# A new opening and a shifted order of reads for an attention block with a Fourier mixer on one core

## The chip, the core and the metric

The kernel runs on one core of a Trainium2 chip. A core has a matrix engine (TensorE, PE in the profile, with its weight loads as PEld), a vector engine (VectorE, DVE), an activation engine (ScalarE, ACT), GpSimd (POOL) and SyncE (SP), which here only issues DMAs. Each engine works through its own instructions in order and waits on semaphores for the others. The data lie in SBUF, matmul results in the eight banks of PSUM, inputs and output in HBM. The metric is the device time of one execution in microseconds (us); the time shown is the median of three runs.

## The reference

There are 8 batches, 8 heads, 512 tokens and 32 state rows of 64 features. Two cross attentions without projections come first: the tokens read the state, and the state reads the tokens. Their outputs, 544 rows per head, go through a real Fourier mix over rows and features, a layer norm without parameters, and a two-layer network with residual.

```python
scores = scale * x @ state.T;  a = softmax(scores);  xread = a @ state      # B, H, 512, D
scores2 = scale * state @ x.T; a2 = softmax(scores2); sread = a2 @ x         # B, H, 32, D
x = concat([xread, sread], axis=2) -> (B, 544, H*D = 512)
u = x + real(fft(fft(x, axis=1), axis=2))
un = (u - mean(u)) / sqrt(var(u) + 1e-6)
out = u + relu(un @ w_ch1) @ w_ch2            # w_ch1 512 x 2048, w_ch2 2048 x 512
```

Inputs and output are float32; the kernel computes its matmuls in bfloat16.

## The kernel before

**Stages of one batch.** `attend(b)` makes the two attentions in 13 steps: turn the state and x on PE (`turn_state`, `turn_x`), scores in both directions with an exponential on ACT (`scores_t`, `scores`), four `xread`s (one matmul pair, then a reciprocal and a multiply on DVE, line 304), `sread` (eight matmuls; a reciprocal; then eight 32-row multiplies that alternate between DVE, line 327, and ACT, line 329, all into the tile XR), `low` (the rows that are their own mirror or fall out of the symmetric blocks), and `fold` (sums and differences of a row and its mirror: Sm, XE, XO, XN). `transform(b)` makes the Fourier mix in 11 steps: four times `over_s` (matmuls with cosine and sine tables over the rows, line 378), two times `over_d` (matmuls with the table T2 over the features, line 391; DVE adds the residual into U), four times `centre` (statistics and subtraction on DVE, lines 233 and 402) and `turn_u` (transposes into unT, line 407). A block of 128 rows and its mirror are computed from the same matmuls; `r` is 0 for a block and 1 for its mirror. `layer1(b)` is 64 matmuls of 512 columns (line 482) with a Relu on ACT; `layer2(b)` is four tiles of 16 matmuls (line 500), each emptied by one DVE operation that scales by the row's standard deviation and adds the residual (`ot`, line 505) and then stored. A mirrored tile goes to a scratch tensor `r_dram` and from there, reversed, to the output (lines 512 and 513); the store waits for the scratch write. `low_rows` and the layers with the key `("L", g)` do the low rows of four batches at once.

**Order.** All five engines run in the order in which the Python code issues instructions. `weave` gives each stream of steps an interval of a stage, spreads the steps evenly over it and issues all by that position; where two are equal the earlier stream goes first. After an opening (tables, `attend(0)`, then `transform(0)` with `attend(1)`), stage `b` weaves `layer1(b)`, `layer2(b - 1)`, `transform(b + 1)` and all of `attend(b + 2)`. The casts of x to bfloat16 are on DVE for batch 0, ACT for batch 1 and POOL after that.

**Buffers.** PSUM has one buffer of two banks for the reads (`psX`, also for `sread`), three banks for all small matmuls (`psQ`), two for layer 1 (tag `ph`) and one for layer 2 (tag `po`); in the last stage every second tile of layer 2 takes a bank of `psQ`. x is loaded in float32 into two buffers `xs` by five DMAs on SyncE's queue; the bfloat16 copies `xin` have two buffers too. `ot` has three.

**Opening.** The tables are computed on DVE (`turn`: an angle reduced to one turn) and ACT (`Sin`), in tiles that share their space with hT. POOL copies the 32-row parts into CL and SL, sets constants in the tiles, and then issues the weight loads, which convert float32 to bfloat16, on a queue of its own (q0; SyncE's DMAs are q1):

```python
    nc.gpsimd.tensor_copy(gate, xs_of[0][:, :, 0])
    for q in range(4):
        nc.gpsimd.dma_start(out=w1[:, :, q * 512:(q + 1) * 512], in_=w1v[:, :, q * 512:(q + 1) * 512])
```

The copy into `gate` makes POOL, and so its loads, wait for x of batch 0.

## Time and profile before

| | |
|---|---|
| median of three runs | 403.11 us (402.58 to 403.5) |
| profiled execution | 403.93 us, of it the span of the trace 402.2 us |
| granted PE clock, mean | 0.939 |
| PE busy | 324.7 us (81%), 1971 matmuls |
| PE weight loads | 174.1 us (43%) |
| DVE busy | 186.7 us (46%) |
| ACT busy | 162.7 us (40%) |
| POOL busy | 60.8 us (15%) |
| HBM read, written | 21.51 MB, 13.11 MB |

Times within a trace count from the start of the span. The profile's page divides the span into 40 equal slices, so a slice is 10 us; a digit is the busy share in tenths. Matmuls are pipelined and their ends are modelled, so a busy PE need not be a PE at its peak. The granted clock (PEclk) is a mean over a window: 1.00 is 2.4 GHz, 0.50 is 1.2 GHz; before its first change it is written as 1.00. In a timeline or a group, `out<-in` names tiles; xin is x in bfloat16, xTp the transposed x in PSUM, xrp, xfp, xlp and srp the reads in PSUM, gp and yp the two transforms, ph and po the layers. A wait is put down to the instruction that released it.

### The profile page before, as it was taken

The numbers are of one execution on the slowest core, as the hardware profiler recorded it, in microseconds if no ns is written. First come the engines' busy times: TensorE is split into PE (matmuls) and PEld (weight loads), VectorE is DVE, ScalarE is ACT, GpSimd is POOL, SyncE is SP. The second block draws the span as 40 slices with busy tenths as digits, with TensorE's granted clock in tenths as the row PEclk, the third lists the DMA queues.
The fourth block names the chain that finished last, engine by engine and source line by source line (L and its number), as shares of the span: only waits on it lengthen the run. The fifth ranks groups of instructions, "written<-read, shape, count | busy, mean of one in ns | idle before, by whom it ended". The sixth has DMA issues, their size and how long they took to land.

```text
span 402.2 us, 5181 instructions
## 1 busy us (share of the span) xinstructions
PE 324.7 (81%) x1971; PEld 174.1 (43%) x2008; DVE 186.7 (46%) x426; ACT 162.7 (40%) x296; POOL 60.8 (15%) x134
## 2 busy tenths in 40 slices
PE   0245649769988998899899996999799999997900
PEld 0123425435544554455564553454445444553400
DVE  8936682683287138733773167415840722001110
ACT  2746326455544454445453523353444353430000
POOL 4680230130022002201220013001200200000000
PEclk9975758999999999999999999899999999999975
DMA  9489963000101610161015110101010111111121
GB/s 190 71 148 196 196 135 61 0 0 2 52 29 52 146 53 13 52 139 47 28 52 133 40 57 35 52 28 52 28 53 28 52 44 63 52 45 39 49 78 52
DMA packets 48744, 26.56 MB, mean 66 GB/s; under 512 B 36176, under 2 KB 44368, under 8 KB 48720
## 3 DMA queue, kind: packets, MB, share of 16 engines
...
q8 instruction: 15, 0.25, 0.3%
q14 instruction: 9, 0.07, 0.1%
HBM read 21.51 MB, written 13.11 MB: 86 GB/s over the span
## 4 chain that ended last, share of the span: by engine, by line
PE 55%; DVE 24%; POOL 4%; ACT 4%; issue 4%; DMA 3%; another core or an unknown queue 1%; SPq 1%; DVEq 0%; ACTq 0%; POOLq 0%
PE ph L482 22%; PE po L500 20%; DVE st L233 3%; PE gp L378 3%; DVE ub L402 3%; DMA out_dram<-ot 3%; DVE ot L505 2%; PE yp L391 2%; DVE XR L327 2%; ACT XR L329 2%; DVE XR L304 2%; PE eTp L276 2%; PE xTp L267 2%; DVE U L395 1%; DVE U L393 1%
## 5 line engine op out<-in xcount | busy, mean ns | idle before, releaser
L500 PE MATMUL po<-w,hT 128*128 128x512 bf16 x501 | 128.4, 381 | 6.2 <-DVE ot L505 5.5
L482 PE MATMUL ph<-unT,w 128*128 128x512 bf16 x491 | 131.0, 384 | 1.1 <-issue 0.2
L484 ACT ACTIVATE hT<-ph 128x512 bf16<-128x512 f32 x128 | 76.5, 597 | 98.0 <-PE ph L482 96.0
L500 PEld LDWEIGHTS <-hT 128*128 128x128 bf16 x512 | 50.2, 98 | 66.4 <-issue 9.1
L482 PEld LDWEIGHTS <-w 128*128 128x128 bf16 x640 | 56.2, 99 | 45.7 <-issue 2.2
L505 DVE SCALAR_TENSOR_TENSOR ot<-po,rstd,U 128x512 f32<-128x512 f32 x32 | 23.9, 750 | 75.1 <-PE po L500 68.0
L393 DVE TENSOR_TENSOR U<-yp,XR 128x511 f32<-128x511 f32 x16 | 10.9, 682 | 47.7 <-PE yp L391 47.7
L237 POOL TENSOR_TENSOR rstd<-mv,epst 128x1 f32<-128x1 f32 x34 | 7.1, 209 | 142.1 <-DVE mv L235 142.1
L409 ACT COPY unT<-tp 128x512 bf16<-128x512 bf16 x32 | 18.7, 584 | 22.1 <-PE tp L407 22.1
L300 PE MATMUL xfp<-stb,ET 128*128 128x260 bf16 x32 | 7.1, 307 | 20.6 <-ACT XR L329 14.2
L233 DVE BATCH_NORM_STATS2 st<-U 128x6 f32<-128x512 f32 x32 | 21.9, 686 | 0.2
L300 PEld LDWEIGHTS <-ET 128*128 128x128 bf16 x80 | 6.4, 100 | 35.7 <-issue 15.1
L385 POOL COPY GL<-G 128x128 bf16<-128x128 bf16 x8 | 2.4, 294 | 126.3 <-ACT G L383 126.3
L383 ACT CAST G<-gp 128x288 bf16<-128x288 f32 x32 | 12.8, 399 | 21.0 <-PE gp L378 15.3
L267 PE MATMUL xTp<-ident,xin 128*128 128x128 bf16 x128 | 11.7, 240 | 11.4 <-DVE xin L111 11.4
L238 POOL TENSOR_TENSOR rstd<-rstd,mhalf 128x1 f32<-128x1 f32 x34 | 20.4, 600 | 2.7
L329 ACT ACTIVATE XR<-srp,rcs 32x64 bf16<-32x64 f32 x32 | 9.9, 310 | 26.0 <-DVE XR L327 26.0
L402 DVE TENSOR_SCALAR ub<-U,mv 128x512 bf16<-128x512 f32 x32 | 16.4, 512 | 1.1
L391 PE MATMUL yp<-T,G 128*128 128x512 bf16 x61 | 16.3, 379 | 0.4 <-ACT E L292 0.2
L267 PEld LDWEIGHTS <-xin 128*128 128x128 bf16 x128 | 9.6, 108 | 14.7 <-DVE xin L111 12.5
L327 DVE TENSOR_SCALAR XR<-srp,rcs 32x64 bf16<-32x64 f32 x32 | 9.0, 281 | 9.9 <-ACT XR L329 9.6
L407 PE MATMUL tp<-ident,ub 128*128 128x128 bf16 x128 | 13.4, 231 | 0.0
...
## 6 DMA issues: line engine op xcount, KB each, us to landing
...
xs<-in_x_dram SPq DMA_DIRECT2D x8, 2.0 KB
```

Of the source, the lines that this page charges most:

```text
L233: nc.vector.bn_stats(st6, u)
L238: nc.gpsimd.tensor_tensor(rstd, rstd, mhalf, op=ALU.pow)
L267: nc.tensor.transpose(p[:, o:o + 128], xin[:, si, 1 + 128 * (2 * g + k):129 + 128 * (2 * g + k)], ident)
L327: nc.vector.tensor_scalar(o, in0=i, scalar1=rcs[ph, g:g + 1], scalar2=None, op0=ALU.mult)
L329: nc.scalar.activation(o, i, AF.Copy, scale=rcs[ph, g:g + 1])
L391: nc.tensor.matmul(yp, lhsT=G[:, c, 128 * k:128 * k + 128], rhs=T2[:, c, :], start=(c == 0), stop=(c == 3))
L402: nc.vector.tensor_scalar(t, in0=ud, scalar1=mv[:, 0:1], scalar2=None, op0=ALU.subtract)
L409: nc.scalar.copy(unT[:, :, col:col + 128], tp[:, 0:512].rearrange("p (a b) -> p a b", b=128))
L482: nc.tensor.matmul(ph[:, o:o + n], lhsT=w1[:, c, f * 128:(f + 1) * 128], rhs=un_of[key][:, c, :], start=(c == 0), stop=(c == DC - 1))
L484: nc.scalar.activation(hT[:, per * i:per * i + per, :].rearrange("p a b -> p (a b)"), ph, AF.Relu)
L500: nc.tensor.matmul(po, lhsT=h_of[key][:, f, i * 128:(i + 1) * 128], rhs=w2[:, f, :], start=(f == 0), stop=(f == FC - 1))
L505: nc.vector.scalar_tensor_tensor(ot, in0=po, scalar=rstd, in1=u, op0=ALU.mult, op1=ALU.add)
```

## The change

- **Weights and x.** POOL's work ahead of `gate` is other work: the table copies into CL and SL move to DVE, and the constants of the state tile move to POOL. x of batch 0 is cast on ACT, of every later batch on POOL. x of batch 2 is loaded after a small DVE copy that stands behind the reads of batch 0.
- **Tables.** The second table is computed for half of its columns only, in three parts that are woven into the opening (`second_turn` on DVE, `second_table` on ACT, `finish_tables` on DVE); the rest is copied with signs. A first `Sin` on a constant stands at the start.
- **Dummy matmuls.** `warm(n)` issues n matmuls of the identity with itself into a PSUM tile that nobody reads: 48 at the start, then 8, 4 or 2 after each step of batch 0's attention and transform.
- **Order.** `attend` returns its scores (seven steps) and its reads (six, with an empty step after `sread`) apart. Batch 1's scores are woven between batch 0's reads. In stage `b` the reads of batch `b + 2` take the first half and the scores of batch `b + 3` the second. Layer 2 is ahead of layer 1 at equal positions.
- **PSUM.** Layer 1, layer 2, the dummies and two of batch 0's reads share one tag `c` with three banks; `sread` uses two tiles of `psQ`, one for each half, with all of DVE's multiplies ahead of ACT's.
- **Layer 1 of batch 0** runs in two halves of 256 columns. Batches 0 and 1 are centred on ACT with the opposite sign, which the Relu's scale turns back.
- **The last batch** has its two mirrored tiles first in layer 2.

```diff
-    psF = ctx.enter_context(tc.tile_pool(name="psF", bufs=2, space=bass.MemoryType.PSUM))
+    psF = ctx.enter_context(tc.tile_pool(name="psF", bufs=3, space=bass.MemoryType.PSUM))
...
-    make_identity(nc, ident)
...
-    pi_ = singles.tile([128, 5], I32, name="pi_")
+    pi_ = singles.tile([128, 4], I32, name="pi_")
...
+    make_identity(nc, ident)
...
         xs, t = xs_of[b], xin_bufs[b % 2]
         if b == 0:
             for si in (0, 1, 3, 2):
-                nc.vector.tensor_copy(t[:, si, 1:513], xs[:, si, :])
-        elif b == 1:
-            for si in (0, 1, 3, 2):
                 nc.scalar.copy(t[:, si, 1:513], xs[:, si, :])
         else:
             nc.gpsimd.tensor_copy(t[:, :, 1:513], xs)
...
+    nc.gpsimd.memset(stb[:, 1:].rearrange("p b g c -> p (b g c)").bitcast(F32), 0.0)
...
-    def state_blocks(lo, hi):
+    def state_blocks(lo, hi, copy=nc.scalar.copy):
...
-            nc.scalar.copy(stb[pq, lo:hi, :, 4 + 64 * hh:68 + 64 * hh], stf[pq, lo:hi, :, :])
+            copy(stb[pq, lo:hi, :, 4 + 64 * hh:68 + 64 * hh], stf[pq, lo:hi, :, :])
...
+    gate = singles.tile([128, 4], F32, name="gate")
+    gate2 = singles.tile([128, 4], F32, name="gate2")
+    nc.vector.memset(gate2, 0.0)
+    nc.scalar.activation(gate2[:, 1:2], gate2[:, 0:1], AF.Sin)
     state_ones(0, 1)
     state_blocks(0, 1)
+    cast_x(0)
...
+    nc.vector.memset(CL.rearrange("p a b -> p (a b)"), 0.0)
+    nc.vector.memset(SL.rearrange("p a b -> p (a b)"), 0.0)
...
+        nc.vector.scalar_tensor_tensor(q, in0=f, scalar=-1.0, in1=f, op0=ALU.mult, op1=ALU.max)
...
+    turned = []
+    def second_turn():
+        nc.vector.tensor_copy(l2, li)
+        turned.extend(turn(dm, dm, l2, [3], gen2))
+    def second_table():
+        f2, q2_ = turned
+        w = 2.0 * PI / dm * shrink
+        nc.scalar.activation(T2[:, 0, :], q2_[:, 0, :], AF.Sin, bias=halfpi, scale=-w)
+        nc.scalar.activation(T2[:, 2, :], f2[:, 0, :], AF.Sin, bias=0.0, scale=-w)
+        nc.scalar.activation(gate2[:, 3:4], gate2[:, 0:1], AF.Exp)
+    def finish_tables():
+        c4 = [T2[:, i, :].rearrange("p (n r) -> p r n", r=4) for i in range(4)]
+        for o, classes in ((1, ((0, 1.0), (2, 1.0), (0, -1.0), (2, -1.0))), (3, ((2, 1.0), (0, -1.0), (2, -1.0), (0, 1.0)))):
+            for r, (i, sign) in enumerate(classes):
+                nc.vector.tensor_scalar(c4[o][:, r, :], in0=c4[i][:, r, :], scalar1=sign, scalar2=None, op0=ALU.mult)
+        alt = T2[0:1, 2, :].rearrange("p (n two) -> p two n", two=2)
+        nc.vector.memset(alt[:, 0, :], 1.0)
+        nc.vector.memset(alt[:, 1, :], -1.0)
+        for hh in range(4):
+            pq = slice(32 * hh, 32 * hh + 32)
+            nc.vector.tensor_copy(CL[pq, hh, :], cl1[pq])
+            nc.vector.tensor_copy(SL[pq, hh, :], sl1[pq])
...
-            (nc.vector.tensor_copy if g == 0 else nc.scalar.copy)(
+            (nc.vector.tensor_copy if g == 0 or b == 0 else nc.scalar.copy)(
...
-        def xread(c0, rev, name, o, ps=slice(0, 128)):
-            p = x2(name)
+        def xread(c0, rev, name, o, ps=slice(0, 128), apart=False):
+            n = ps.stop - ps.start
+            p = None if apart else x2(name)
+            rs = wk.tile([128, 2, 4], F32, name="rs", tag="rs", bufs=4)
+            ov = o.rearrange("p (g h d) -> p g h d", g=2, d=D)
             for half in range(2):
                 g = 1 - half if rev else half
                 rhs = sb[:, g, 259::-1] if rev else sb[:, g, 4:264]
-                nc.tensor.matmul(p[:, half, 0:260], lhsT=ET[:, g, c0:c0 + 128], rhs=rhs, start=True, stop=True)
-            n = ps.stop - ps.start
-            rs = wk.tile([128, 2, 4], F32, name="rs", tag="rs", bufs=4)
+                ph = psF.tile([128, 512], F32, name=name, tag="c") if apart else p[:, half]
+                nc.tensor.matmul(ph[:, 0:260], lhsT=ET[:, g, c0:c0 + 128], rhs=rhs, start=True, stop=True)
+                if apart:
+                    nc.vector.reciprocal(rs[ps, half], ph[ps, 256:260])
+                    nc.vector.tensor_tensor(
+                        ov[:, half], in0=ph[ps, 0:256].rearrange("p (h d) -> p h d", d=D),
+                        in1=rs[ps, half].unsqueeze(2).to_broadcast([n, 4, D]), op=ALU.mult)
+            if apart:
+                return
             nc.vector.reciprocal(rs[ps], p[ps, :, 256:260])
             nc.vector.tensor_tensor(
-                o.rearrange("p (g h d) -> p g h d", g=2, d=D),
-                in0=p[ps, :, 0:256].rearrange("p g (h d) -> p g h d", d=D),
-                in1=rs[ps].unsqueeze(3).to_broadcast([n, 2, 4, D]),
-                op=ALU.mult,
-            )
+                ov, in0=p[ps, :, 0:256].rearrange("p g (h d) -> p g h d", d=D),
+                in1=rs[ps].unsqueeze(3).to_broadcast([n, 2, 4, D]), op=ALU.mult)
 
 
         def sread():
-            p = x2("srp")
+            rcs = wk.tile([128, 2], F32, name="rcs", tag="rcs")
             for g in range(2):
+                p = qt("srp")
                 for si in range(4):
-                    nc.tensor.matmul(p[:, g, 0:257], lhsT=E[:, si, g, :], rhs=xin[:, si, 257 * g:257 * g + 257],
+                    nc.tensor.matmul(p[:, 0:257], lhsT=E[:, si, g, :], rhs=xin[:, si, 257 * g:257 * g + 257],
                                      start=(si == 0), stop=(si == 3))
-            rcs = wk.tile([128, 2], F32, name="rcs", tag="rcs")
-            nc.vector.reciprocal(rcs, p.rearrange("p g c -> p (g c)")[:, 0:769:768])
-            for hh in range(4):
-                for g in range(2):
+                nc.vector.reciprocal(rcs[:, g:g + 1], p[:, 256 * g:256 * g + 1])
+                for hh in range(4):
                     c0 = 512 - (256 * g + 64 * hh)
                     ph = slice(32 * hh, 32 * hh + 32)
                     o = XR[0:32, 0, c0:c0 - 64:-1]
-                    i = p[ph, g, 1 - g + 64 * hh:65 - g + 64 * hh]
+                    i = p[ph, 1 - g + 64 * hh:65 - g + 64 * hh]
...
-        return [
+        first = [
             turn_state,
...
+        ]
+        second = [
             lambda: xread(256, True, "xrp", XR[:, 0, 1:513]),
             sread,
-            lambda: xread(0, False, "xfp", XF[:, 0, 0:512]),
+            None,
+            lambda: xread(0, False, "xfp", XF[:, 0, 0:512], apart=(b == 0)),
             low,
-            lambda: xread(128, False, "xfp", XF[:, 1, 0:512]),
+            lambda: xread(128, False, "xfp", XF[:, 1, 0:512], apart=(b == 0)),
             lambda: (xread(384, True, "xrp", XR[:, 1, 1:513]), fold()),
         ]
+        return first, second
     un_of, tiles_of = {}, {}
+    flipped = (0, 1)
...
+        order = [(0, 1), (1, 1), (0, 0), (1, 0)] if b == B - 1 else [(0, 1), (0, 0), (1, 1), (1, 0)]
...
-            nc.vector.tensor_scalar(t, in0=ud, scalar1=mv[:, 0:1], scalar2=None, op0=ALU.subtract)
+            if b in flipped:
+                nc.scalar.activation(t, ud, AF.Identity, bias=mv[:, 0:1], scale=-1.0)
+            else:
+                nc.vector.tensor_scalar(t, in0=ud, scalar1=mv[:, 0:1], scalar2=None, op0=ALU.subtract)
...
-            col = (2 * k + 1 - r) * 128
+            col = order.index((k, r)) * 128
...
-            for k in range(2):
-                for r in (1, 0):
+            for k, r in order:
+                if True:
...
-            ph = psF.tile([128, 512], F32, name="ph", tag="ph")
+            ph = psF.tile([128, 512], F32, name="ph", tag="c")
...
+        def half_step(i, r):
+            ph = psF.tile([128, 512], F32, name="ph", tag="c")
+            cols = slice(256 * r, 256 * r + 256)
+            for f in (2 * i, 2 * i + 1):
+                for c in range(DC):
+                    nc.tensor.matmul(ph[:, 256 * (f % 2):256 * (f % 2) + 256], lhsT=w1[:, c, f * 128:(f + 1) * 128],
+                                     rhs=un_of[key][:, c, cols], start=(c == 0), stop=(c == DC - 1))
+            nc.scalar.activation(hT[:, 2 * i:2 * i + 2, cols], ph.rearrange("p (a b) -> p a b", b=256), AF.Relu,
+                                 scale=-1.0 if key in flipped else 1.0)
+        if key == 0:
+            return [lambda i=i, r=r: half_step(i, r) for r in range(2) for i in range(FC // 2)]
...
-                po_of[i] = (psQ if last and i % 2 else psF).tile(
-                    [128, dm], F32, name="po", tag="q" if last and i % 2 else "po", bufs=3 if last and i % 2 else 1)
+                po_of[i] = psF.tile([128, dm], F32, name="po", tag="c")
...
-    cast_x(0)
-    weave((attend(0), 0, 1))
-    nc.vector.memset(alt[:, 0, :], 1.0)
-    nc.vector.memset(alt[:, 1, :], -1.0)
-    nc.gpsimd.memset(stb[:, 1:].rearrange("p b g c -> p (b g c)").bitcast(F32), 0.0)
+    def warm(n):
+        t = psF.tile([128, 512], F32, name="warm", tag="c")
+        for i in range(n):
+            nc.tensor.matmul(t[:, 0:128], lhsT=ident, rhs=ident, start=(i == 0), stop=(i == n - 1))
+    def warmed(steps, n):
+        return [lambda s=s: (s(), warm(n)) for s in steps if s is not None]
+    warm(48)
+    s0, r0 = attend(0)
+    s1, r1 = attend(1)
+    weave((warmed(s0, 8), 0, 1), ([second_turn], 0.5, 0.5))
     state_ones(1, B)
-    state_blocks(1, B)
+    state_blocks(1, 2)
     cast_x(1)
+    weave((warmed(r0, 4), 0, 1), (s1, 0.35, 1.2), ([second_table], 0.36, 0.36), ([finish_tables], 0.9, 0.9))
+    nc.vector.tensor_copy(gate2[:, 0:1], xs_of[0][:, 0, 0:1])
     load_x(2)
-    weave((transform(0), 0, 1), (attend(1), 0, 1))
-    for b in range(B + 1):
-        streams = []
+    state_blocks(2, B, nc.gpsimd.tensor_copy)
+    weave((warmed(transform(0), 2), 0, 1), (r1[:1], 0.1, 0.1), (r1[1:2], 0.75, 0.75))
+    s2, r2 = attend(2)
+    s3, reads_next = attend(3)
+    weave((layer1(0), 0, 1), (r1[2:], 0, 0.35), (transform(1), 0.35, 1.0), ([lambda: cast_x(2)], 0, 0), (s2, 0.15, 0.55), (r2, 0.55, 1.1),
+          ([lambda: load_x(3)], 0.2, 0.2), ([lambda: cast_x(3)], 0.7, 0.7), (s3, 0.75, 1.1), ([lambda: load_x(4)], 0.8, 0.8))
+    for b in range(1, B + 1):
+        low = layer2(("L", b // 4 - 1)) if b in (4, 8) else []
+        streams = [(low + layer2(b - 1), 0, 1)]
         if b < B:
             streams.append((layer1(b), 0, 1))
-        if b > 0:
-            low = layer2(("L", b // 4 - 1)) if b in (4, 8) else []
-            streams.append((low + layer2(b - 1, last=(b == B)), 0, 1))
         if b + 1 < B:
             streams.append((transform(b + 1), 0.04, 0.97))
         if b + 2 < B:
-            streams.append(([lambda: cast_x(b + 2)], -0.1, -0.1))
-            streams.append((attend(b + 2), 0, 0.95))
+            streams.append((reads_next, 0, 0.5))
         if b + 3 < B:
-            streams.append(([lambda: load_x(b + 3)], 0, 0.1))
+            scores_next, reads_next = attend(b + 3)
+            streams.append(([lambda: cast_x(b + 3)], 0.3, 0.3))
+            streams.append((scores_next, 0.5, 1))
+        if b + 4 < B:
+            streams.append(([lambda: load_x(b + 4)], 0.35, 0.35))
         if b in (3, 7):
             streams.append((low_rows(b // 4), 0.05, 0.5))
             streams.append((layer1(("L", b // 4)), 0.55, 1))
```

## Rows read from the trace of the kernel before

**Rows 1.** Page, the span in 40 slices, tenths busy, TensorE.
```profile
PE   0245649769988998899899996999799999997900
```

**Rows 2.** Busy time by stage: window, length, engines' busy time, PEclk, DMA share, GB/s.
```profile
58.90:90.00 31.10, 25.22 (x163) 14.18 (x166) 18.49 (x44) 16.51 (x32) 5.32 (x10) 0.93 0.17 32
90.00:213.00 123.00, 115.23 (x749) 63.63 (x761) 66.02 (x147) 56.80 (x105) 16.98 (x32) 1.00 0.20 54
213.00:259.00 46.00, 42.17 (x244) 21.96 (x248) 21.35 (x47) 17.71 (x33) 5.32 (x10) 0.96 0.22 63
259.00:363.40 104.40, 101.01 (x582) 51.74 (x593) 34.95 (x77) 43.85 (x78) 7.73 (x20) 1.00 0.13 46
363.40:367.89 4.49, 3.40 (x15) 1.55 (x16) 0.73 (x2) 0.00 (x0) 0.00 (x0) 1.00 0.17 64
```

**Rows 3.** Waits of PE, 58.9 to 368: total us, times, longest.
```profile
PE xfp L300 <- ACT XR L329: 8.2, 6, 3.2
PE po L500 <- DVE ot L505: 6.1, 6, 2.8
PE xfp L300 <- DVE XL L304: 4.2, 4, 1.1
```

**Rows 4.** Timeline of PE: start, length, line, operation, what ended the idle time.
```profile
35.87 0.66 PE L378 MATMUL gp<-CT,XE 128*128 128x288 bf16 x2 [1.87 <-DVE XE L339]
...
59.10 0.63 PE L482 MATMUL ph<-unT,w 128*128 128x512 bf16 x1
```

**Rows 5.** Busy time by stage, the first loads: last columns DMA share, GB/s.
```profile
0.00:7.10 7.10, 0.79 (x4) 0.34 (x4) 5.34 (x24) 2.46 (x5) 4.78 (x20) 1.00 0.80 157
10.00:11.00 1.00, 0.00 (x0) 0.00 (x0) 1.00 (x3) 0.49 (x1) 0.00 (x0) 1.00 1.19 236
11.00:13.50 2.50, 0.00 (x0) 0.00 (x0) 2.40 (x4) 2.49 (x5) 0.00 (x0) 1.00 1.18 197
```

**Rows 6.** Timeline of POOL in the opening.
```profile
15.09 1.32 POOL L199 CAST CL<-gen 32x288 bf16<-32x288 f32 x1
...
17.02 0.52 POOL L199 CAST CL<-gen 32x288 bf16<-32x288 f32 x1
...
21.34 3.18 POOL L221 DMA_DIRECT2D w<-in_moe_w_ch_dram  x4
...
55.38 1.89 POOL L116 CAST xin<-xs 128x2048 bf16<-128x2048 f32 x1
```

**Rows 7.** DMA queues (packets, MB, share): 23 to 24, then 26 to 50.
```profile
q0 software_dynamic: 26, 0.03, 28.7%
...
q0 software_dynamic: 3745, 3.72, 91.2%
...
q1 hardware_dynamic: 3790, 0.96, 30.0%
```

**Rows 8.** DVE by line: count, busy us, mean ns of one, idle before.
```profile
L233 DVE BATCH_NORM_STATS2 st<-U 128x6 f32<-128x512 f32 x32 | 21.9, 686 | 0.2
...
L393 DVE TENSOR_TENSOR U<-yp,XR 128x511 f32<-128x511 f32 x16 | 10.9, 682 | 47.7 <-PE yp L391 47.7
...
L327 DVE TENSOR_SCALAR XR<-srp,rcs 32x64 bf16<-32x64 f32 x32 | 9.0, 281 | 9.9 <-ACT XR L329 9.6
...
L235 DVE BATCH_NORM_AGGREGATE mv<-st 128x2 f32<-128x6 f32 x34 | 6.2, 182 | 3.0
...
L304 DVE TENSOR_TENSOR XL<-xlp,rs 32x512 bf16<-32x512 f32 x8 | 5.5, 687 | 0.3
...
L338 DVE TENSOR_TENSOR Sm<-XF,XR 128x1028 bf16<-128x1028 bf16 x8 | 5.6, 695 | 0.8
```

**Rows 9.** Timeline of the tail, DVE and SyncE.
```profile
367.89 0.75 DVE L505 SCALAR_TENSOR_TENSOR ot<-po,rstd,UL 128x512 f32<-128x512 f32 x1 [3.76 <-remote]
...
382.44 0.63 SPq L513 DMA_DIRECT2D out_dram<-r_dram  x1
...
391.84 0.61 SPq L513 DMA_DIRECT2D out_dram<-r_dram  x1
```

More of the change, by code (lines that the diff above doesn't have):

```diff
@@ L147 @@
     w2v = moe_w_ch2.rearrange("(c p) f -> p c f", p=128)
-    gate = singles.tile([128, 4], F32, name="gate")
-    gate2 = singles.tile([128, 4], F32, name="gate2")
-    CT = singles.tile([128, 2, NM], BF16, name="CT")
-    ST = singles.tile([128, 2, NM], BF16, name="ST")
-    CL = singles.tile([128, 4, NM], BF16, name="CL")
-    SL = singles.tile([128, 4, NM], BF16, name="SL")
-    T2 = singles.tile([128, 4, dm], BF16, name="T2")
-    nc.gpsimd.memset(CL.rearrange("p a b -> p (a b)"), 0.0)
-    nc.gpsimd.memset(SL.rearrange("p a b -> p (a b)"), 0.0)
@@ L160 @@
-    pf = singles.tile([128, 5], F32, name="pf")
-    l1, l2 = gen1[:, 4096 - NM:], gen2[:, 4096 - dm:]
-    nc.vector.tensor_copy(pf, pi_)
-    for hh in range(4):
-        nc.vector.memset(pf[32 * hh:32 * hh + 1, 2:3], 0.0)
-    nc.vector.tensor_copy(l1, lt)
-    nc.vector.memset(l1[:, 256:257], 0.0)
-    nc.vector.tensor_copy(l2, li)
-    def turn(W, N, lf, cols, scratch):
-        n = len(cols)
-        f = scratch[:, 0:n * W].rearrange("p (n w) -> p n w", w=W)
-        q = scratch[:, n * W:2 * n * W].rearrange("p (n w) -> p n w", w=W)
-        for i, c in enumerate(cols):
-            nc.vector.tensor_scalar(f[:, i, :], in0=lf, scalar1=pf[:, c:c + 1], scalar2=None, op0=ALU.mult)
-        nc.vector.tensor_scalar(q, in0=f, scalar1=1.0 / N, scalar2=float(1 << 23), op0=ALU.mult, op1=ALU.add)
-        nc.vector.tensor_scalar(q, in0=q, scalar1=float(1 << 23), scalar2=-float(N), op0=ALU.subtract, op1=ALU.mult)
-        nc.vector.tensor_add(f, f, q)
-        nc.vector.tensor_scalar(q, in0=f, scalar1=-1.0, scalar2=None, op0=ALU.mult)
-        nc.vector.tensor_max(q, q, f)
-        return f, q
@@ L192 @@
-    w = 2.0 * PI / dm * shrink
-    nc.scalar.activation(T2[:, 0:2, :], q2_, AF.Sin, bias=halfpi, scale=-w)
-    nc.scalar.activation(T2[:, 2:4, :], f2, AF.Sin, bias=0.0, scale=-w)
-    nc.scalar.activation(gate2[:, 0:1], epst, AF.Exp)
-    alt = T2[0:1, 2, :].rearrange("p (n two) -> p two n", two=2)
-    for hh in range(4):
-        pq = slice(32 * hh, 32 * hh + 32)
-        nc.gpsimd.tensor_copy(CL[pq, hh, :], cl1[pq])
-        nc.gpsimd.tensor_copy(SL[pq, hh, :], sl1[pq])
     def two(name, shape):
@@ L216 @@
     GLs = [singles.tile([128, 4, 128], BF16, name=f"GL{i}") for i in range(2)]
+    CT = singles.tile([128, 2, NM], BF16, name="CT")
+    ST = singles.tile([128, 2, NM], BF16, name="ST")
+    CL = singles.tile([128, 4, NM], BF16, name="CL")
+    SL = singles.tile([128, 4, NM], BF16, name="SL")
+    T2 = singles.tile([128, 4, dm], BF16, name="T2")
+    nc.vector.memset(CL.rearrange("p a b -> p (a b)"), 0.0)
+    nc.vector.memset(SL.rearrange("p a b -> p (a b)"), 0.0)
+    pf = singles.tile([128, 4], F32, name="pf")
@@ new lines, with turn @@
+    l1, l2 = gen1[:, 4096 - NM:], gen2[:, 4096 - dm:]
+    cl1 = gen1[:, 2048:2048 + NM // 2].bitcast(BF16)
+    sl1 = gen1[:, 2560:2560 + NM // 2].bitcast(BF16)
+    def turn(W, N, lf, cols, scratch):
+        n = len(cols)
+        f = scratch[:, 0:n * W].rearrange("p (n w) -> p n w", w=W)
+        q = scratch[:, n * W:2 * n * W].rearrange("p (n w) -> p n w", w=W)
+        for i, c in enumerate(cols):
+            nc.vector.tensor_scalar(f[:, i, :], in0=lf, scalar1=pf[:, c:c + 1], scalar2=None, op0=ALU.mult)
+        nc.vector.tensor_scalar(q, in0=f, scalar1=1.0 / N, scalar2=float(1 << 23), op0=ALU.mult, op1=ALU.add)
+        nc.vector.tensor_scalar(q, in0=q, scalar1=float(1 << 23), scalar2=-float(N), op0=ALU.subtract, op1=ALU.mult)
+        nc.vector.tensor_add(f, f, q)
+        nc.vector.scalar_tensor_tensor(q, in0=f, scalar=-1.0, in1=f, op0=ALU.mult, op1=ALU.max)
+        return f, q
@@ new lines @@
+    shrink = 1.0 - 1e-6
+    nc.vector.tensor_copy(l1, lt)
+    nc.vector.memset(l1[:, 256:257], 0.0)
+    nc.vector.tensor_copy(pf, pi_)
+    for hh in range(4):
+        nc.vector.memset(pf[32 * hh:32 * hh + 1, 2:3], 0.0)
+    f1, q1 = turn(NM, Stot, l1, [0, 1, 2], gen1)
+    w = 2.0 * PI / Stot * shrink
+    nc.scalar.activation(CT, q1[:, 0:2, :], AF.Sin, bias=halfpi, scale=-w)
+    nc.scalar.activation(ST, f1[:, 0:2, :], AF.Sin, bias=0.0, scale=w)
+    nc.scalar.activation(cl1, q1[:, 2, :], AF.Sin, bias=halfpi, scale=-w)
@@ new lines @@
+    nc.scalar.activation(sl1, f1[:, 2, :], AF.Sin, bias=0.0, scale=w)
+    nc.scalar.activation(gate2[:, 2:3], gate2[:, 0:1], AF.Exp)
+    turned = []
[8 more added lines that the diff above has]
+        nc.scalar.activation(gate2[:, 3:4], gate2[:, 0:1], AF.Exp)
```

26 lines of the change are left out of this document (9 added, 17 removed).

## The prediction

> **What bounds the kernel now.** I read four views: the busy slices, the busy time by stage, TensorE's waits, and the chain of waits at both ends. The slices [rows 1] split the run in three: TensorE (PE) works little in the first six slices, is nearly full in the middle, and stops two slices before the end.
>
> The middle begins with the first layer-1 matmul at 59.1 us [rows 4] and, for my sum, runs from 58.9 to 367.9 us, where the output of the last low rows starts on VectorE (DVE) [rows 9]. By stage [rows 2] PE is busy 287.0 of these 309.0 us, so idle for 22.0. The granted clock costs more: 31.1 us at a mean of 0.93 lose 2.2, and 46.0 at 0.96 lose 1.8. What is left, 309.0 - 22.0 - 4.0 = 283.0 us, is matmul work at full clock; it can't be hidden. The idle time has three main names [rows 3]: the read matmuls behind the XR chain that goes back and forth between DVE and ScalarE (ACT) (8.2 us), the layer-2 tile behind the one buffer that DVE empties (6.1), the reads behind XL (4.2). All are one crowding: in a stage the reads of one batch and the centring of another fall into the same half on DVE.
>
> The opening, 58.9 us, is a chain over DVE, GpSimd (POOL), ACT and PE. The tail, 34.3 us from the low rows' output to the end, is DMA: the first reversed store is issued at 382.4, the second, which waits for a scratch write queued behind it, at 391.8, and the span ends at 402.2 [rows 9].
>
> **The opening, part by part.** Tables, warm matmuls and casts before about 20 us change places, but none decides: the next thing does.
>
> The weights are issued by POOL. Before, that came at 21.3 us [rows 6], because POOL stood behind the table copies; x of batches 0 and 1 had gone through by 13.5 [rows 5]. Afterwards POOL has no table copies, and its issue waits for x of batch 0 alone. By 7.1 us 7.1 x 157 = 1.11 MB have moved [rows 5], which is state 0 and x of batch 0 (0.07 + 1.05 MB); with some 0.4 for landing (an estimate) the gate opens at 7.5. Before, 2.4 us passed from the issue at 21.34 to the first weight packets, which appear in the window 23 to 24 [rows 6, 7]. So weights could flow from 10.0. POOL's small casts, though, took 1.32 us beside DVE's table arithmetic and 0.52 after it [rows 6], and now DVE does tables until about 16; I take 1 us for that and let them flow from 11.0 (bounds 10.0 and 13.5).
>
> At 11.0 x of batch 1 still lacks 2.5 x 197 = 0.49 MB, at 10.0 another 0.24 [rows 5]. Beside the weights, x loads (256-byte pieces) got 0.96 MB in 24 us, 40 GB/s, packet for packet with the weights' 3.72 MB [rows 7]. So x of batch 1 lands at 11.0 + 0.49/0.040 + 0.4 = 23.7 us; from 10.0 it would be 28.6, from 13.5 no later than now. The Trainium skill says in "DMA: Bandwidth & Descriptors", section "Queues, rings and completion order", that each DMA engine goes round-robin between its queues packet by packet. That speaks against this change, and the trace agrees (3790 packets to 3745); without it the same bytes would need 2 us and the sum would be case B below.
>
> This matters because the transposes of batch 1's x now stand on PE, in the written order, ahead of batch 0's low read, its last two reads and its fold. PE takes them in order. From the landing: POOL's cast 1.9 [rows 6] and 0.1 to start, so 25.7. Then transposes 0.9 (estimate, eight at half clock), 0.2 latency, DVE's copy 0.7 (as wide as Sm), low read 0.9 plus three small operations 0.55, the read split in halves 1.2 (between 0.9 for one piece and 1.8 for two full ones), the finish of the tables 4.1 (eight quarter-width multiplies at 0.2, two memsets 0.54, eight 32-row copies at 0.25; estimates from the XL and XR rows), the last read 0.9, Sm 0.7, XE 0.4 (half as wide as Sm) [rows 8]: 10.6. The first transform matmul starts at 36.3; before it was 35.9 [rows 4], so by then nothing is won.
>
> From there to layer 1: four first-transform groups with their ACT copies 4.2, second transform 0.9, U 1.4, two statistics 1.7 (0.69 and 0.18 each), second U 1.4, a third 0.85, the DVE part of sread 1.4, a fourth 0.85, centring now on ACT 0.7, transposes 0.5 (DVE's parts from [rows 8], the rest estimates from the same stretch): 13.9. Layer 1 starts at 50.2 instead of 58.9. This is where the opening gains: half of batch 1's reads no longer stand between, and centring leaves DVE. Weights (eight transfers of 0.52 MB at 3.72 MB in 24 us) are in by 11 + 27 = 38, so they hold nothing.
>
> **The dummy matmuls** cost PE some 0.1 us each at half clock; the first 48 are done by about 9, under the table arithmetic on DVE, the others in waits. I cost them at nothing (bounds 0 and 3 us: 8 after each of seven steps, if every one fell on the chain). The higher clock gives back at most the 2.2 us above; I keep 1.2 of loss at the start of layer 1 and 1.3 later.
>
> **The stages.** Work left at layer 1 is 283.0 plus four reads of batch 1, 0.9. The XR wait goes: sread has two PSUM buffers of its own, and an empty step (0.07 of a 37 us stage) follows it. The layer-2 tile now takes a free third buffer; what is late next is the layer-1 tile that gets the old one, 0.9 us later, and DVE is emptier there, since reads (8.5 us of DVE work by the same durations) and centring (7) lie in opposite halves. The reads behind XL keep their distance of 2.6 us and stay in part; POOL's cast, now amid the reads, still slows XE. The stage of batch 0 is dense: about 23 us on DVE beside 26 on PE; I leave it 4 us idle, and the others 4 together. Idle and clock are then 8.0 + 2.5 = 10.5 instead of 26.0.
>
> **The tail.** The last batch puts its two reversed tiles first. SyncE's queue is in order: scratch write, wait, reversed store, again, and each reversed store holds the next write for 9.4 us [rows 9]. Both chains still follow the low rows; the direct stores only move behind. I take 0, bounds -1 and +1.3.
>
> **Sum.** 50.2 + 283.9 + 10.5 = 344.6 for the low rows, + 34.3 = 378.9, and 1.7 outside the span (403.9 - 402.2) = 380.6. The profiled execution lies 0.8 above the median of the three runs (403.9 against 403.1), so 380 us.
>
> **Rivals.**
> - B: x of batch 1 is not late. If DVE holds POOL back until x is through (13.5), the opening runs at DVE's pace: tables and first copies to 12.3, second table 3.9 and eight memsets to 16.8, then its part of reads, copies and finished tables 13.3 (the pieces above, with the first read 0.9, sread 1.4 and batch 1's state copy 0.4), so 30.1 for the first transform, 44.0 for layer 1, 6.2 sooner: 374. For it: POOL's slowed casts [rows 6]. Against: the weight issue is only eight instructions of 0.8 us. The Trainium skill, "SBUF — State Buffer", section "SBUF: two separate sides", says that DVE's fast two-port operations lock POOL out from writing the descriptors of its DMAs; by that rule B would hold, and no row of this kernel shows such a DMA held back.
> - D: x of batch 1 lands after all weights: 38 + 0.49/0.2 + 0.4 = 40.9, that is 17.2 later, 397. Against: the even packet count [rows 7].
> - C: the guard and order do what they say, but idle time in the stages only changes its name (DVE's queue stays the last to end): 15.5 more, 395. For: DVE is as busy as before in sum.
> - S, slower: with one PSUM tag, a layer-1 tile that directly follows a finished layer-2 tile gets that tile's buffer and waits for its output operation. Such a wait was 6.1/6 = 1.0 us in the trace [rows 3]. At each of the 28 tile ends of seven stages that is 28 us: 408. It is slower from 24 such ends on. Against: a buffer whose Relu is long done is usually free.
> - That the change doesn't do what it says is D in part: the guard protects x of batch 0 and lets the weights meet x of batch 1.
>
> **How the numbers follow.** Forecast 0.52, its own range 374 to 387 (weights from 13.0 to 10.0, idle 8 to 13). B 0.15, C 0.15, D 0.08, S 0.07, and 0.03 for C and part of D together, about 403. A measurement here tells 0.2% (0.8 us) from no change. Faster holds the forecast, B, C and D: 0.90; same 0.03; slower 0.07. The range 370 to 398 leaves out S, the 0.03, and the far ends of B and C, under 0.2 in all.
>
> **What would show it.** First weight packets near 11 us, x of batch 1 landing near 24, and PE waiting there in the transposes of xin for POOL's cast: steps of the opening right. First layer-1 matmul at 50 (44: B; 66: D). No wait of xfp for XR, and few of po for ot; if instead ph waits for ot after each tile, S. PE idle in the middle below 10 us; if it is near 20, C. A tail of 34 us from the low rows' output; if it is shorter by several us, the tail step was wrong. The whole is wrong if layer 1 starts after 59.

## The result, and the profile after

The changed kernel takes 381.3 us (median of 4 runs, 380.9 to 382.1) against 402.9 (402.6 to 403.5): a ratio of 0.946 (95% interval 0.944 to 0.949). The profiled execution took 382.1 us with a span of 380.3. Line numbers are those of the changed kernel from here on, and under an experiment those of its own kernel.

TensorE in the 40 slices of the page, which answers to [rows 1]: the hole of the opening has partly filled (with dummies too), and the middle is nearly without gaps.

```profile
PE   6736768979999999999999999999999999989900
```

PE's timeline (start, length, line, operation, what ended the idle time) and POOL's, for [rows 4, 6]:

```profile
25.10 1.04 PE L283 MATMUL xTp<-ident,xin 128*128 128x128 bf16 x8 [7.78 <-POOL xin L113]
...
35.29 0.66 PE L406 MATMUL gp<-CT,XE 128*128 128x288 bf16 x2 [3.59 <-DVE XE L360]
...
51.32 1.05 PE L523 MATMUL ph<-unT,w 128*128 128x256 bf16 x5
```
```profile
8.35 0.35 POOL L235 COPY gate<-xs 128x4 f32<-128x4 f32 x1 [0.15 <-DMA xs<-in_x_dram]
8.90 3.18 POOL L237 DMA_DIRECT2D w<-in_moe_w_ch_dram  x4 [0.20 <-issue]
12.03 3.01 POOL L239 DMA_DIRECT2D w<-in_moe_w_ch_dram  x4
23.15 1.89 POOL L113 CAST xin<-xs 128x2048 bf16<-128x2048 f32 x1 [8.11 <-DMA xs<-in_x_dram]
```

The weights leave at 8.9 in place of 21.3, POOL then waits 8.1 us for x of batch 1, PE waits for POOL's cast, and layer 1 starts at 51.3, 7.8 us earlier. Queues between 14.0 and 23.1 (packets, MB, share), for [rows 7]:

```profile
q0 software_dynamic: 1542, 1.53, 100.1%
q1 hardware_dynamic: 1056, 0.26, 22.2%
```

The middle by stage (window, length, busy time of PE, PEld, DVE, ACT, POOL, then PEclk, DMA share, GB/s), for [rows 2]; and PE's waits between 51.3 and 346.8, for [rows 3]:

```profile
51.30:75.00 23.70, 21.96 (x197) 17.38 (x194) 11.97 (x33) 13.20 (x27) 1.63 (x5) 0.93 0.24 46
75.00:85.00 10.00, 7.41 (x90) 6.32 (x91) 8.65 (x20) 9.31 (x18) 5.87 (x9) 1.00 0.00 0
85.00:190.00 105.00, 104.52 (x668) 57.24 (x667) 62.81 (x149) 47.75 (x93) 14.57 (x31) 1.00 0.25 71
190.00:235.00 45.00, 44.21 (x291) 24.25 (x289) 20.33 (x48) 20.35 (x40) 5.62 (x11) 1.00 0.10 38
235.00:338.60 103.60, 102.23 (x578) 51.36 (x577) 34.35 (x75) 41.68 (x78) 7.71 (x20) 1.00 0.14 50
```
```profile
PE ph L513 <- ACT hT L515: 2.1, 4, 0.7
PE po L543 <- ACT hT L515: 1.4, 2, 0.7
PE xrp L320 <- DVE XF L329: 1.3, 2, 0.8
```

PE is idle 8.3 us between 51.3 and the low rows' output at 346.8 (295.4 - 287.1), where it was 22.0. Both names at the head of [rows 3], XR and ot, are gone; 85 to 190 us is full but for 0.5 us. So 7.6 us came from the opening (58.9 to 51.3), 13.6 from the middle (309.0 to 295.4), and 0.8 from the tail (34.3 to 33.5). The tail, DVE and SyncE, for [rows 9]:

```profile
346.76 0.75 DVE L548 SCALAR_TENSOR_TENSOR ot<-po,rstd,UL 128x512 f32<-128x512 f32 x1 [4.41 <-PE po L543]
...
361.16 1.41 DVE L548 SCALAR_TENSOR_TENSOR ot<-po,rstd,U 128x512 f32<-128x512 f32 x2 [6.80 <-DMA out_dram<-ot]
```
```profile
350.94 1.76 SPq L555 DMA_DIRECT2D r_dram<-ot  x1
361.33 0.62 SPq L556 DMA_DIRECT2D out_dram<-r_dram  x1
...
369.67 0.61 SPq L556 DMA_DIRECT2D out_dram<-r_dram  x1
```

### The profile page after: what moved, and what is told of

The parts are those of the page before. It is cut to its first block, busy times and chain, and to the rows that moved or that the text cites. A ratio compares the mean times of both kernels' runs of the same rounds, so it can differ in the third digit from the quotient of the medians.

```text
span 380.3 us, 5665 instructions
## 1 busy us (share of the span) xinstructions
PE 331.0 (87%) x2222; PEld 190.3 (50%) x2222; DVE 177.3 (47%) x444; ACT 161.4 (42%) x306; POOL 58.7 (15%) x129
## 4 chain that ended last, share of the span: by engine, by line
PE 68%; DVE 13%; DMA 7%; ACT 3%; SPq 2%; issue 1%; POOL 1%; DVEq 0%; POOLq 0%; ACTq 0%
PE ph L513 25%; PE po L543 25%; DMA xs<-in_x_dram 4%; PE gp L406 4%; PE yp L419 3%; DMA out_dram<-ot 3%; DVE st L249 2%; PE ph L523 2%; SPq L104 1%; DVE U L421 1%; PE tp L438 1%; DVE U L423 1%; PE srp L339 1%; ACT hT L515 1%; PE xTp L283 1%
## 5 line engine op out<-in xcount | busy, mean ns | idle before, releaser
L515 ACT ACTIVATE hT<-ph 128x512 bf16<-128x512 f32 x112 | 66.9, 597 | 126.1 <-PE ph L513 126.0
L513 PE MATMUL ph<-unT,w 128*128 128x512 bf16 x448 | 115.0, 379 | 0.0
L513 PEld LDWEIGHTS <-w 128*128 128x128 bf16 x576 | 51.4, 98 | 55.2 <-issue 2.9
L543 PEld LDWEIGHTS <-hT 128*128 128x128 bf16 x512 | 48.4, 98 | 46.1 <-issue 1.0
L283 PE MATMUL xTp<-ident,xin 128*128 128x128 bf16 x128 | 10.9, 230 | 9.5 <-POOL xin L113 8.8
L575 PE MATMUL warm<-ident 128*128 128x128 bf16 x150 | 15.4, 253 | 3.3 <-POOL halfpi L78 3.3
L523 PE MATMUL ph<-unT,w 128*128 128x256 bf16 x128 | 17.9, 289 | 0.0
L438 PE MATMUL tp<-ident,ub 128*128 128x128 bf16 x128 | 12.4, 219 | 5.8 <-ACT ub L431 4.5
L575 PEld LDWEIGHTS <-ident 128*128 128x128 bf16 x150 | 12.7, 116 | 5.1 <-POOL halfpi L78 3.3
L350 ACT ACTIVATE XR<-srp,rcs 32x64 bf16<-32x64 f32 x32 | 9.9, 309 | 11.8 <-DVE rcs L341 11.5
L438 PEld LDWEIGHTS <-ub 128*128 128x128 bf16 x128 | 9.5, 98 | 10.6 <-ACT ub L431 6.5
## 6 DMA issues: line engine op xcount, KB each, us to landing
w<-in_moe_w_ch_dram POOLq DMA_DIRECT2D x8, 512.0 KB, 15.4
```

The lines of the kernel that those rows point to most:

```text
L283: nc.tensor.transpose(p[:, o:o + 128], xin[:, si, 1 + 128 * (2 * g + k):129 + 128 * (2 * g + k)], ident)
L438: nc.tensor.transpose(tp[:, 128 * j:128 * j + 128], ub[k, r][:, 128 * j:128 * j + 128], ident)
L513: nc.tensor.matmul(ph[:, o:o + n], lhsT=w1[:, c, f * 128:(f + 1) * 128], rhs=un_of[key][:, c, :], start=(c == 0), stop=(c == DC - 1))
L515: nc.scalar.activation(hT[:, per * i:per * i + per, :].rearrange("p a b -> p (a b)"), ph, AF.Relu, scale=-1.0 if key in flipped else 1.0)
L523: nc.tensor.matmul(ph[:, 256 * (f % 2):256 * (f % 2) + 256], lhsT=w1[:, c, f * 128:(f + 1) * 128], rhs=un_of[key][:, c, cols], start=(c == ...
L543: nc.tensor.matmul(po, lhsT=h_of[key][:, f, i * 128:(i + 1) * 128], rhs=w2[:, f, :], start=(f == 0), stop=(f == FC - 1))
```

## Experiments

Each ran three rounds beside the kernel before on the same chip (403.7 to 404.1 there). The changed kernel's own ratio is 0.946 on one chip and 0.945 on another.

### The opening: x of batch 1 ahead of the weights

```diff
     nc.gpsimd.tensor_copy(gate, xs_of[0][:, :, 0])
+    cast_x(1)
     for q in range(4):
         nc.gpsimd.dma_start(out=w1[...], ...)
```
(and the later `cast_x(1)` goes)

> The changed kernel (381.3 us), with POOL casting x of batch 1 ahead of its weight loads, so that the weights also wait for x of batch 1. Theory (the weights starve x of batch 1, and PE and DVE wait for it): the cast runs at about 14 instead of 23 us, DVE no longer stands still from 20 to 26 us, the first transform matmul comes about 6 us sooner (near 29 instead of 35.3) and the total falls by 5 to 7, to about 375.5. Rival 1 (x of batch 1 was late, but ACT's second table holds batch 1 as long): 0 to 2 sooner, 379 to 381. Rival 2 (the weights, now 7 us later, hold x of batch 2 or layer 1 in its place): no gain or slower, 381 or more, with PE waiting for xin or ph waiting for w near 45 us.

Measured: 377.1 us, 0.933 (0.931 to 0.934), 5.2 us less by the ratio. POOL's timeline, then PE's:

```profile
15.96 1.90 POOL L113 CAST xin<-xs 128x2048 bf16<-128x2048 f32 x1 [7.16 <-DVE rs L329]
17.79 3.18 POOL L238 DMA_DIRECT2D w<-in_moe_w_ch_dram  x4
```
```profile
29.98 0.66 PE L407 MATMUL gp<-CT,XE 128*128 128x288 bf16 x2 [3.77 <-DVE XE L361]
...
45.95 1.34 PE L524 MATMUL ph<-unT,w 128*128 128x256 bf16 x6
```

The cast is 7.2 us earlier, the first transform and layer 1 are 5.3 earlier, and the middle is as long as it was. So in the changed kernel the weights do hold up x of batch 1, and through it the opening. The first transform at 30.0 is what case B gave for an opening at DVE's pace (30.1); layer 1 at 46.0 is 2.0 later than case B gave.

### The dummy matmuls

```diff
     def warm(n):
+        return
```

> The changed kernel without any of the 150 dummy matmuls. My step had them at nothing on the chain, and worth a little clock: 381 to 383. Rival 1 (they cost, because PE has to get through them between the steps): 1 to 3 us faster, 378 to 380. Rival 2 (the clock that they keep up carries the opening): 3 us or more slower, 384 or more, with the granted clock low through the transform of batch 0 and the first stage.

Measured: 381.2 us, 0.942 (0.940 to 0.945), layer 1 at 51.1. The 150 dummies (15.4 us of busy PE) neither cost nor give anything that can be told.

### The order of the stages

```diff
-    s3, reads_next = attend(3)
...
-            streams.append((reads_next, 0, 0.5))
+            streams.append(([lambda: cast_x(b + 2)], -0.1, -0.1))
+            first, second = attend(b + 2)
+            streams.append((first + [s for s in second if s is not None], 0, 0.95))
...
-            scores_next, reads_next = attend(b + 3)
-            streams.append(([lambda: cast_x(b + 3)], 0.3, 0.3))
-            streams.append((scores_next, 0.5, 1))
```
(scores and reads of a batch in one stage again, loads and casts with them)

> The changed kernel with the old order of the stages: from stage 1 on the whole attention of batch b + 2 lies in one stage (13 steps over 0 to 0.95, no empty step), with cast and load where they were before; PSUM tags, opening and sread stay as changed. Theory (the crowding of reads and centring on DVE made PE wait): PE idle in the stages comes back in good part, 5 to 9 us, total 386 to 390, with waits of reads for XF or XL. Rival (the PSUM buffers of sread and the shared tag did it): 0 to 2 us, 381 to 383. In this kernel batch 3's scores also leave the first stage, which by itself should give back up to 1 us there.

Measured: 388.1 us, 0.960 (0.957 to 0.962). Layer 1 starts where it did (50.6), but the middle takes 300.7 us with 13.3 idle. PE's waits:

```profile
PE xfp L320 <- DVE XL L329: 2.7, 3, 1.0
PE xrp L320 <- DVE XF L329: 2.7, 2, 2.2
PE po L543 <- ACT hT L515: 2.3, 4, 0.7
```

The order is worth 5 to 6 us: the reads wait for one another again. No wait for XR is among them: the read's own two tiles keep it away in the old order too.

### One PSUM tile for both groups of the first read

```diff
+            p = x2("srp")
             for g in range(2):
-                p = qt("srp")
```

> The changed kernel with sread as before: one two-bank tile shared with the reads, and multiplies that alternate between DVE and ACT. Theory (the order with its empty step gives the chain the room that it needs): 0 to 3 us, about 382.5, with at most short waits of xfp for XR outside the opening. Rival (the two PSUM tiles of its own were what removed the 8.2 us of that wait): 5 to 9 us, 386 to 390, with the wait of xfp for XR back in every stage.

Measured: 385.4 us, 0.952 (0.948 to 0.956). The interval overlaps that of the changed kernel a little. By the trace layer 1 is 1.4 us later (52.7) and the middle 2.0 longer (297.4). The first is not the tile's: x of batch 1 was cast at 25.6 here, 2.5 later. xfp does not wait for XR in the stages here either: in the new order the tile's place is free in time, so the two single buffers are worth some 2 us beside it, and not the 8.2 of [rows 3]. Either edit takes that wait away without the other; with both undone (under "The opening alone") it is back, 5.0 us in 5 waits.

### The PSUM tag

```diff
-    psF = ctx.enter_context(tc.tile_pool(name="psF", bufs=3, ...))
+    psF = ctx.enter_context(tc.tile_pool(name="psF", bufs=2, ...))
-                po_of[i] = psF.tile([128, dm], F32, name="po", tag="c")
+                po_of[i] = psF.tile([128, dm], F32, name="po", tag="po", bufs=1)
```

> The two layers get their own PSUM tags again, two banks for layer 1 and one for layer 2, with the rest of the change kept. Theory that the one tag takes away the waits of layer 2's tile for the copy of the output (6.1 us before, none after): they come back, 2 to 6 us, and the time is 383 to 387 us. Rival, that in the new order of the stages the work beside the tiles covers the copy: 381 us within 1, with waits po<-ot under 1 us. Rival, that the one tag costs by waits of layer 1's tile (ph<-hT 2.1 us, po<-hT 1.4 us after): 378 to 380 us.

Measured: 393.7 us, 0.974 (0.970 to 0.978): 11.5 us slower than with one tag, twice the upper end of what I expected. PE's waits between 51.3 and 360 us; then DVE's timeline before one of them; then busy time by stage around it (columns as above):

```profile
PE po L543 <- DVE ot L548: 11.7, 6, 2.7
```
```profile
143.51 0.69 DVE L329 TENSOR_TENSOR XR<-xrp,rs 128x512 bf16<-128x512 f32 x1
144.31 0.69 DVE L359 TENSOR_TENSOR Sm<-XF,XR 128x1028 bf16<-128x1028 bf16 x1
145.04 0.43 DVE L360 TENSOR_TENSOR XE<-Sm 128x512 bf16<-128x512 bf16 x1
145.38 0.42 DVE L361 TENSOR_TENSOR XO<-Sm 128x510 bf16<-128x510 bf16 x1
145.72 0.17 DVE L362 COPY XN<-Sm 128x2 bf16<-128x2 bf16 x1
145.79 0.74 DVE L548 SCALAR_TENSOR_TENSOR ot<-po,rstd,U 128x512 f32<-128x512 f32 x1
```
```profile
136.00:143.80 7.80, 7.80 (x41) 3.92 (x40) 4.11 (x12) 2.18 (x4) 0.29 (x1) 1.00 0.37 95
143.80:146.60 2.80, 0.14 (x2) 0.01 (x1) 2.66 (x7) 0.60 (x1) 0.00 (x0) 1.00 0.84 190
146.60:149.50 2.90, 2.90 (x10) 1.16 (x10) 1.23 (x3) 0.00 (x0) 0.79 (x2) 0.61 0.30 105
```

The output operation ot stands in DVE's queue behind a read's row work, and with one bank for layer 2 the next tile waits for it, 2.7 us here. After the wait the granted clock falls to a mean of 0.61, between its levels of 2.4 and 1.2 GHz, so 2.9 us lose another 1.1. Over the middle PE is idle 16.1 us (309.55 - 293.43) in place of 8.3, and the same matmuls keep it busy 6.3 us longer (293.4 to 287.1), with a granted clock of 0.96 from 100 to 220 us where the changed kernel has 1.00. Idle time and the clock behind it are each about half of the price. In the kernel before the same number of waits came to 6.1 us [rows 3]: with one bank they are longer here.

### The tag alone, in the kernel before

```diff
-            ph = psF.tile([128, 512], F32, name="ph", tag="ph")
+            ph = psF.tile([128, 512], F32, name="ph", tag="c")
```
(with three banks in `psF`, and po in the same tag, in the last stage too)

> The kernel before, with one edit: one PSUM tag of three banks for both layers in place of two banks and one. Theory that layer 2's tile waits for a copy that stands in DVE's queue behind a read's row work, and the one tag takes that wait away in the old order as well: the 6.1 us of waits po<-ot go and so does the half clock after them; 394 to 398 us. Rival, that in the old order PE then waits for the reads instead (xfp<-XR 8.2 us grows by what the tag frees): 402 to 405 us. Rival, that layer 1's tile waits for ot in the tag: over 405 us.

Measured: 400.0 us, 0.990 (0.987 to 0.993): 3.7 us faster, between the theory and its rival. PE's waits between 51 and 370 us, and the first of them in the same window before the change:

```profile
PE xfp L300 <- ACT XR L329: 11.5, 7, 3.3
PE xfp L300 <- DVE XL L304: 4.3, 4, 1.3
...
PE po L499 <- ACT hT L484: 2.1, 3, 0.7
```
```profile
PE xfp L300 <- ACT XR L329: 11.3, 7, 3.2
```

The wait for ot is gone in the old order too. The waits for XR do not grow: one of the seven, of some 3 us, lies ahead of layer 1 in both kernels, and from layer 1 on they are 8.2 us in 6, as in [rows 3]. So the rival's mechanism does not come, and PE's idle time in the middle falls by 6.9 us, from 22.0 to 15.0 (304.19 - 289.15). But the middle is only 4.6 shorter (308.8 to 304.2, from the first layer-1 matmul), for PE is busy 2.3 us longer with the same work. Its stretch from 80 to 100 us (columns as above), here and before the change:

```profile
80.00:100.00 20.00, 17.97 (x103) 9.76 (x103) 11.75 (x27) 10.63 (x20) 3.43 (x5) 0.83 0.00 1
```
```profile
80.00:100.00 20.00, 16.23 (x107) 9.06 (x109) 11.92 (x26) 10.80 (x21) 3.43 (x5) 1.00 0.00 1
```

The granted clock is 0.83 in place of 1.00, so in this execution part of what the tag freed goes to the clock. Whether the other executions lose it in the same place is not shown. Layer 1's tile never waits for ot, so rival S falls in both orders.

### The opening alone

```diff
-                p = qt("srp")
+            p = x2("srp")
...
-                po_of[i] = psF.tile([128, dm], F32, name="po", tag="c")
+                po_of[i] = psF.tile([128, dm], F32, name="po", tag="po", bufs=1)
...
-            streams.append((reads_next, 0, 0.5))
+            streams.append((first + [s for s in second if s is not None], 0, 0.95))
```
(order, read's tile and tags together as before the change)

> Order of the stages, one PSUM tile for both groups of the reads, and two PSUM tags as before the change; only the new opening is kept. Theory that the parts of the stages add up (the order alone cost 5 us of idle time, the read's tile 2 to 3 us, the tags 2 to 6 us): 390 to 395 us, with 14 to 18 us idle in the middle. Rival, that the order alone made the difference and the others follow from it: 388 us within 1, idle 13 us.

Measured: 401.1 us, 0.992 (0.989 to 0.995), slower than expected: the expectation had the tags at 2 to 6 us. Against the changed kernel's 0.945 it is 0.047 x 403.8 = 18.9 us. Taken out one at a time, order (0.960), tile (0.952) and tags (0.974) cost 5.5, 2.3 and 11.5 us against the mean of the changed kernel's two ratios (0.946) or its own, 19.3 together: from this side the parts add. From the other side they don't: opening alone 3.2 us, tag alone 3.7, the whole 22. And the opening alone keeps only 3.2 of the 7.6 us that the traces show for it. Its profiled execution lies 4.7 us above the median, about as much as its layer 1 is late (56.2 against 51.3; x of batch 1 was cast at 27.9). The middle behind it (columns as above):

```profile
56.18:370.64 314.46, 291.22 (x1856) 160.46 (x1854) 142.59 (x318) 134.31 (x254) 36.47 (x73) 0.99 0.17 50
```

That is 5.5 us longer than the 309.0 before the change: PE is busy 4.2 us longer (291.2 to 287.0) and idle 1.2 longer. By this one trace, what the opening gives is lost again in the middle. Part of it is work that the new opening leaves to the middle: in the changed kernel 285.4 us at full clock, 283.0 before. Where the rest comes from stays open; these stages are not quite the old ones, for layer 2 is still issued ahead of layer 1 at equal positions.

### The tail: the low rows last

```diff
-        streams = [(low + layer2(b - 1), 0, 1)]
+        streams = [(layer2(b - 1) + low if b == B else low + layer2(b - 1), 0, 1)]
```

> In the last stage the second layer of batch 7 runs before that of the 31 low rows, so that the low rows' small stores leave last. Theory that the end is set by the stores behind the low rows' output (33.5 us from that output to the end, of which 10.65 us lie in the low rows' own transfers, ahead of the reversed stores): the reversed stores start earlier by the low rows' work and the end comes 4 to 8 us earlier, 374 to 377 us. Rival, that the reversed stores' own chain sets the end wherever the low rows stand: 381 us within 1. Rival, that the low rows' transfers then end last and alone: 383 to 389 us.

Measured: 380.4 us, 0.942 (0.939 to 0.945), no difference that counts. SyncE issued the reversed stores 12 us earlier:

```profile
349.18 0.62 SPq L556 DMA_DIRECT2D out_dram<-r_dram  x1
...
357.87 0.62 SPq L556 DMA_DIRECT2D out_dram<-r_dram  x1
```

Then the low rows' stores ended last and alone (25 GB/s between 370 and 375 us). Whichever stands behind the other pays.

### The tail: stores of 31 rows cut in two

```diff
-                dst.append((slice(32 * bq + 1, 32 * bq + 32), out[b, 257:288, :]))
+                dst.append((slice(32 * bq + 1, 32 * bq + 17), out[b, 257:273, :]))
+                dst.append((slice(32 * bq + 17, 32 * bq + 32), out[b, 273:288, :]))
```

> The changed kernel, with each store of 31 low rows (62 KB) cut in two, of 16 and of 15 rows; nothing else. In the changed kernel the last four of these stores move 25 GB/s for 10 us, the fourth ot waits 6.8 us for them, and the first reversed store is issued only after them. Theory that a store of 31 rows goes through one DMA engine and holds up the end: with 16 and 15 rows they are through in 2 to 3 us, the wait of ot goes, and the end comes 7 to 12 us earlier: 369 to 374 us. Rival, that the reversed stores (two of 256 KB at 50 GB/s, one after the other) set the end anyway: 378 to 381 us. Rival, that 15 and 16 rows take no more engines than 31: 381 us, or 382 by four more issues on SP.

Measured: 376.7 us, 0.931 (0.928 to 0.934), 5.8 us less by the ratio: less than the theory's 7 to 12, and below the rivals. In the profiled execution ot has no wait for a store, and low rows to end take 26.8 us (376.6 - 349.8) in place of 33.5. Its x of batch 1 came late (layer 1 at 54.7), so the tail's 6.7 us are not all in the time.

### Both together, and the reversed stores in four pieces

> The changed kernel with x of batch 1 cast ahead of the weights' loads (which gave 5 us by the trace) and the low rows' stores cut in 16 and 15 rows. Theory that opening and tail add: the gain of the cut alone plus 4 to 5 us, 364 to 370 us. Rival, that an earlier middle runs into the stores of the tail in the same place: 374 to 377 us.

Measured: 369.1 us, 0.913 (0.911 to 0.916). Layer 1 starts at 44.6, low rows to end take 26.4 us: the gains add. With the last edit on top:

```diff
-                    out=out[b, top:top - 128:-1, :].rearrange("r (c n) -> c r n", c=2),
+                    out=out[b, top:top - 128:-1, :].rearrange("r (c n) -> c r n", c=4),
```
(and the same for the source)

> The version of e13 (369.1 us) with the reversed stores in four pieces of a row (512 bytes) in place of two (1 KB); the first piece index stays the outermost dimension. Theory that each piece has a DMA engine of its own (two pieces move 49 GB/s, one store of 31 rows moved 25 GB/s, so an engine moves 25 GB/s): four pieces move near 100 GB/s, the two reversed stores of the last batch take 2.6 us each in place of 5.2 us, and the end comes 3 to 6 us earlier: 363 to 366 us. Rival, that the pieces of 512 bytes move at half the rate on each engine: 369 us within 1. Rival, that four engines under the stores slow x's loads or the packets of the weights in the middle: 369 to 373 us.

Measured: 364.5 us, 0.901 (0.899 to 0.904), the fastest version here. Stretches of the tail in which one store moves alone, the last number GB/s: 31 rows and two pieces in the changed kernel, then four pieces in this one.

```profile
355.00:360.00 5.00, 5.00 (x25) 2.26 (x24) 0.00 (x0) 0.00 (x0) 0.00 (x0) 1.00 0.07 25
...
364.50:368.00 3.50, 0.00 (x0) 0.00 (x0) 0.00 (x0) 0.00 (x0) 0.00 (x0) 0.65 0.14 49
```
```profile
353.20:354.00 0.80, 0.80 (x6) 0.33 (x5) 0.00 (x0) 0.00 (x0) 0.00 (x0) 1.00 0.29 94
```

Undoing the order of the last batch's tiles was not tried, nor were layer 2 ahead of layer 1, the halves of batch 0's layer 1, or the centring on ACT by themselves.

## Why the prediction was right, step by step

- **Weights and x of batch 1.** The first weight packet was forecast at 11.0 and came between 11.7 and 11.8 (8 by 12.0), behind an issue at 8.90 that I had at 7.5; x of batch 1 was forecast at 23.7, and POOL's cast, which waits for it, started at 23.15. Two errors cancel here, and that is luck. By 12.0 the loads' queue had moved 2.31 of the 2.63 MB that it had moved at the cast, so 0.32 MB were open, not 0.49. Those came at 29 GB/s (0.32 in 11.1 us), not at 40. The two queues between 13 and 15 us, then between 16 and 21:

```profile
q0 software_dynamic: 353, 0.35, 112.4%
q1 hardware_dynamic: 51, 0.01, 4.6%
```
```profile
q0 software_dynamic: 779, 0.78, 91.6%
q1 hardware_dynamic: 779, 0.20, 29.9%
```

From 16 to 21 the packets are even and the loads get 40 GB/s, as forecast and as the round-robin that I took from the Trainium skill has it. The forecast lacked the start, where the weights moved 353 packets and the loads 51; why is not shown. The experiment on the opening shows the delay. Case B's mechanism, weights held back until 13.5, did not come: the first packet came 2.8 to 2.9 us after the issue, and 2.0 to 2.1 before the change (between 23.3 and 23.4, so my 2.4 was read too late). Of the lock that the Trainium skill names for it ("SBUF — State Buffer", "SBUF: two separate sides") no more than these 0.8 us can be in it; I had allowed 1.
- **To the first transform.** 12.6 us forecast from the landing, 12.1 measured (23.15 to 35.29).
- **To layer 1.** 13.9 forecast, 16.0 measured. PE waits for the centring on ACT and for XR, 1.8, 1.2 and 2.3 us ahead of the tp transposes. The term had the centring on ACT (0.7) and DVE's part of sread (1.4), but not what stands ahead of the last centring in ACT's queue: ACT's own four multiplies of sread (1.27 us from 48.29) and a copy into unT (0.58). The centring's statistics were done at 49.2, and it started at 50.2.
- **Middle.** Idle and clock 10.5 forecast; 8.3 idle and 1.7 of clock measured (23.7 us at 0.93). Work 283.9 forecast; 285.4 measured (287.1 - 1.7). No wait for XR and none for ot, as forecast. The forecast gave the end of the wait for XR to the read's tiles and the empty step together; the runs show that either is enough. What it did not see is how little the waits of [rows 3] say of prices. The wait behind the read's tile was the largest (8.2 us), and the tile is worth some 2 beside the new order; the order is worth 5.5; and the tag, with waits of 6.1, is the dearest part, 11.5 us, since in the new order one bank for layer 2 brings waits of 11.7 us and a lower clock behind them. Alone it gave 3.7: the waits went, and in the profiled execution a third of the 6.9 us of idle time that this saved came back as longer busy time. The forecast of the sum came out right, without the parts' prices behind it.
- **Tail.** 34.3 forecast as unchanged, 33.5 measured. I saw that both reversed chains follow the low rows, and did not ask why those stores last: 10.65 us in the chain for 31-row stores at 25 GB/s, ahead of the reversed ones, holding the fourth ot for 6.8 us.
- **Dummies.** Nothing forecast, nothing measured.
- **Sum.** 51.3 + 295.4 + 33.5 = 380.3: +1.1, +1.0 and -0.8 against the terms of the forecast, which came to 378.9.
